# A half tile of w1 shared by pairs of outputs in 64-row tiles, PSUM given out as eight single banks, and norms on two engines

## The chip, the cores and the metric

The kernel runs on one core of a Trainium2 chip. A core has five engines that run their own instruction streams and wait for each other by semaphores: TensorE (PE, matrix products into PSUM), VectorE (DVE), ScalarE (ACT), GpSimd (POOL) and SyncE (SP), which here issues transfers. PSUM, where matrix products end, has eight banks of 128 rows x 512 fp32 values. The metric is the device time of one execution in microseconds; the median of three runs of the kernel before is 190.47 us (190.22 to 190.83).

## What is computed

A block of a transformer over 2048 tokens of width 448, with norms whose scale and shift come from a condition vector. Attention has 16 heads of width 28 and looks at 8 positions, two apart. The MLP has 1792 hidden units. Cut to what matters:

```python
mod = (silu(c) @ w_mod).reshape(1, 6, 1, 448)          # sa, ca, ga, sb, cb, gb
h = layernorm(x) * (1 + ca) + sa
q, k, v = split(h @ wqkv)                               # 16 heads of 28
attn = softmax over idx = pos - 2 * arange(8), masked   # per position
x = x + ga * (attend(attn, v) @ wo)
h = layernorm(x) * (1 + cb) + sb
y = layernorm(h)
x = x + gb * (gelu(y @ w1 + b1) @ w2 + b2)
```

## The kernel before

Tokens are laid out so that even ones come first, then odd ones: the distance of two becomes a distance of one. There are 16 blocks of 128 tokens. The width of 448 makes four k-tiles, the last of them half full: 3 x 128 + 64 rows. The bias b1 stands in row 64 of the last k-tile of `w1_s` (`KA`), against a column of ones in `ybufs`; the rest of that tile is zero.

The whole program is a list of named operations, each with its engine (or a choice of two), a planned duration, what it needs and which buffers it takes. `Plan.order` (L99) walks through them with a planner's clock and always takes the operation that could start first, corrected by priorities (`PRI`, `NUDGE`, `LOOK`). The order of instructions on every engine is what comes out; it is fixed when the program is built. PSUM is three pools with turns in them (`SLOTS`): `lt`, two buffers of two banks, `s`, three of one bank, and `p2`, one bank.

The operations, with their names in the plan and their lines:

- `fst`, `frs`, `z`, `zt`, `h` (`front_end`, L491): statistics of x, 1/sqrt(variance) on GpSimd (L416), the norm (L421, VectorE only), the transposition (L517 on PE for blocks 0 to 7, by a transfer for the rest), scale and shift into `hT` (L526, L529).
- `qk`, `qe` (L539, L386, L384): q and k of two or four blocks, 8 outputs of 4 matmuls, copied out by ScalarE or VectorE.
- `lt`, `ex`, `mk`, `pv`, `ve`, `po`, `rd`, `on`, `pt`, `ot` (`attention`, L598) for each of 17 groups of 121 positions. `lt` is 16 matmuls of 28 rows, placed at row 32*r of the array, into two buffers of two banks; `ex` is two exponentials over 1024 columns each (L624); `mk` masks; `po` multiplies by v; `on` divides.
- `wo`, `x1` (L700, L705): the output product and the addition to x.
- `s2`, `r2`, `z2`, `ml`, `ad`, `s3`, `r3`, `y`, `yt` (`norm_items`, L707): the two norms ahead of the MLP, for pairs of blocks, and a transposing transfer of `ybuf` into `yT` (L739).
- `w1`, `ge` (`mlp_items`, L744), for four chunks of four blocks: 7 steps of two outputs, 4 matmuls of 128 x 512 each (L755), then one gelu over both banks (L762).
- `w2`, `fin`, `out` (L778, L791, L793): the second product, two matmuls a step and block, the additions, and the output transfer.
- `ps_sa`, `ps_ca`, `mod1`, `pb_ga` to `pb_gb` (L453 to L462, L563): the condition's six vectors. Where the last k-tile has 64 rows, matmuls of 64 rows or columns stand between ones of 128.
- `idle` (L325): matmuls on zeros while the first loads are under way.

Of the kernel before, what the change touches and what calls it, by code (L numbers as in the profile page):

```python
# [15 lines left out]
DP = 512  # L16
KT = 4
KA = 64
# [16 lines left out]
SLOTS = {"lt": 2, "s": 3, "p2": 1, "et": 2, "on": 2, "vb": 3, "z2": 2, "yT": 2, "hm": 2}  # L35

LANDS = [("c", 3.0), ("x0", 5.0), ("x2", 5.8), ("wmsa", 6.4), ("wmca", 7.2), ("wk", 8.4), ("wq", 9.4), ("later", 10.0),
         ("wv", 10.4), ("x4", 12.5), ("wmod2", 18.0), ("wo", 19.5), ("b2", 20.5), ("x8", 22.0), ("w1", 28.0),
         ("w2", 33.0)]

NIDLE = [11, 4]
PLANS = None

LOOK = 0.000121

PRI = {"ad": -181.5, "agfst": -82.1, "ags2": -347.3, "ex": -137.9, "ge": -154.4, "h": -94.5, "lt": 209.3,
       "mk": -29.7, "ml": 177.8, "on": -459.2, "po": -127.9, "pv": -157.8, "r2": 73.3, "r3": -46.8, "s2": -114.2,
       "s3": -56.5, "ve": 41.4, "w1": -75.6, "w2": -12.0, "wo": 472.9, "wq": 377.0, "x1": 437.8, "y": -137.1,
       "yt": 24.4, "z": -134.6, "z2": 11.3, "zt": 143.7}

NUDGE = {"ad12": 15.6, "ad2": -30.3, "ad8": 44.8, "agfst12": -48.8, "agfst6": 98.9, "ags2_13": -79.7,
       "ags2_14": 66.3, "ags2_15": -24.2, "ags2_2": 13.3, "ags2_8": 84.1, "ags3_13": 100.2, "ags3_14": -12.2,
       "ex14.1": 144.5, "fin2": 21.9, "ge2.0": -4.6, "ge3.3": -73.9, "h2.2": 280.0, "lt10": 82.1, "lt8": -96.4,
       "mk16": -4.1, "mk3": 236.6, "ml0": 45.3, "ml12": 24.2, "ml6": -123.2, "on16": -89.1, "on4": -65.7,
       "on9": 60.2, "ot11": 20.9, "ot2": 66.5, "ot3": -126.0, "ot4": -23.7, "out1": 36.4, "out14": 29.2,
       "out15": -322.5, "out2": 24.7, "out9": -87.4, "po16": 38.4, "po9": 49.4, "pt16": 16.3, "pt2": 36.7,
       "pt3": -118.5, "pv13": -326.1, "pv16": 12.1, "qe0.0": 77.8, "qe0.6": -60.5, "qe12.5": 124.2,
       "qe2.5": 111.3, "qe8.0": 142.3, "qe8.3": 117.4, "qk2.5": 255.7, "qk8.0": 142.4, "qk8.1": 138.6,
       "r2_10": 7.9, "r2_12": 207.3, "r2_14": 18.8, "r2_14a": 2.8, "r2_4a": 155.1, "r2_8": -68.9, "r2_8a": 87.6,
       "r3_0a": -13.7, "r3_10a": -65.1, "r3_12": -63.0, "r3_12a": 43.9, "r3_14": 28.5, "r3_14a": -10.2,  # L60
       "r3_8": -10.6, "rd15": 41.6, "rd16": -89.1, "s2_1": 61.5, "s2_12": -57.7, "s2_13": -42.9, "s2_15": -4.9,
       "s2_3": 68.8, "s2_9": -35.4, "s3_12": 65.1, "s3_14": 46.0, "w1_0.6": 31.3, "w1_1.5": 58.9,
       "w1_3.3": -59.1, "w2_0.6": 121.6, "w2_1.4": 61.0, "w2_11.0": 60.4, "w2_11.3": -105.2, "w2_11.4": -4.4,
       "w2_11.5": 45.1, "w2_11.6": 30.7, "w2_12.5": -140.6, "w2_13.2": -158.9, "w2_14.1": -6.6, "w2_14.3": -1.2,
       "w2_14.4": 47.8, "w2_14.5": 147.1, "w2_2.5": 20.1, "w2_4.2": -47.2, "w2_5.2": -7.0, "w2_5.3": -24.7,
       "w2_5.5": 19.2, "w2_5.6": -17.6, "w2_6.1": 3.9, "w2_6.2": 12.3, "w2_6.6": 5.9, "w2_8.0": -68.8,
       "w2_8.3": -69.5, "w2_8.5": 91.6, "w2_9.3": 69.1, "wo1": 88.2, "wo12": -28.3, "wo2": 44.1, "x1_1": 34.4,
       "x1_13": -39.6, "x1_3": -114.7, "y1": 51.8, "y10": 10.9, "y12": 102.0, "y13": -21.9, "y14": 13.4,
       "y3": 128.0, "yt12": -52.1, "yt13": 30.6, "yt14": 12.1, "yt9": 260.3, "z2_1": 79.9, "z2_12": 15.9,
       "z2_13": 66.8, "z2_14": 106.9, "z2_15": 45.5, "z2_4": 123.4, "z2_6": -29.2}  # L70
# [9 lines left out]
class Plan:  # L80
# [8 lines left out]
    def add(self, name, eng, needs=(), after=(), uses=(), allocs=(), lag=0.09, tab=None, at=0.0, fn=None, pri=0.0):  # L89

        i = len(self.ops)
        self.index[name] = i
        self.ops.append(dict(name=name, eng=eng, needs=list(needs), after=list(after), allocs=list(allocs), lag=lag,
                             tab=tab, at=at, fn=fn, pri=pri + PRI.get(re.match(r"[a-z]+([0-9](?=_))?", name)[0], 0.0) +
                             NUDGE.get(name, 0.0)))
        for b in list(uses) + list(allocs):
            self.bufs[b][1].append(i)

    def order(self, hop=0.07, table=1.3, win=3.413):  # L99
# [27 lines left out]
        tab = None  # L127
# [6 lines left out]

        def slot_time(t, extra=0):
            k = len(turn[t]) + extra - self.slots[t]
            if k < 0:
                return 0.0
            b = turn[t][k] if k < len(turn[t]) else None
            if b is None or any(end[u] is None for u in users[b]):  # L140
                return None
            return max(end[u] for u in users[b]) + hop

        while ready:
            best = None
            for i in ready:
# [7 lines left out]
                ok, cntt = True, {}  # L154
                for b in o["allocs"]:
                    tg = tag_of[b]
                    st = slot_time(tg, cntt.get(tg, 0))
                    cntt[tg] = cntt.get(tg, 0) + 1
                    if st is None:
                        ok = False  # L160
                        break
                    t = max(t, st)
# [4 lines left out]
                s = max(t, free[e])  # L167
# [3 lines left out]
                if best is None or key < best[0]:  # L171
                    best = (key, i, e, s)
            assert best is not None, [ops[i]["name"] for i in ready]
            _, i, e, s = best
            o = ops[i]
            d = o["eng"][e]
            if e == "PE":
                w = int(s / win)
# [11 lines left out]
            for b in o["allocs"]:  # L190
                turn[tag_of[b]].append(b)
# [14 lines left out]
def kernel(  # L206
# [39 lines left out]

    cst = ctx.enter_context(tc.tile_pool(name="cst", bufs=1))
    ps_lt = ctx.enter_context(tc.tile_pool(name="ps_lt", bufs=2, space=bass.MemoryType.PSUM))
    ps_s = ctx.enter_context(tc.tile_pool(name="ps_s", bufs=SLOTS["s"], space=bass.MemoryType.PSUM))
    ps_p2 = ctx.enter_context(tc.tile_pool(name="ps_p2", bufs=SLOTS["p2"], space=bass.MemoryType.PSUM))  # L250

    def ps_att(shape, dtype, name):
        return ps_s.tile(shape, dtype, name=name, tag="s")

    ps_small = ps_att
# [35 lines left out]
    b2_bc = cst.tile([128, D], BF16, name="b2_bc")  # L291
    silu_bf = cst.tile([128, KT], BF16, name="silu_bf")
# [9 lines left out]
    wmod = stp.tile([128, KT, 2, D], BF16, name="wmod")  # L302
    wqk_st = stp.tile([128, KT, 2 * D], BF16, name="wqk_st")
    nc.scalar.dma_start(out=x_all[:, 0:2, :], in_=xv[:, 0, 0:2, :])
    load_ktiles(nc.sync, wmod[:, :, 0, :], w_mod[:, 0:D], 0)
    load_ktiles(nc.scalar, wmod[:, :, 1, :], w_mod[:, D:2 * D], 0)
# [7 lines left out]
    nc.sync.dma_start(out=b2_bc[:], in_=B_b2.partition_broadcast(128))  # L314
    nc.sync.dma_start(out=x_all[:, 8:NBLK, :], in_=xv[:, 1, :, :])
# [6 lines left out]
    def idle(n):  # L322
        for i in range(n):
            idle_ps = ps_att([128, 512], FP32, "idle_ps")
            nc.tensor.matmul(idle_ps[:], lhsT=idle_in[:, 0:128], rhs=idle_in[:], start=True, stop=True)  # L325

    idle(4)
# [5 lines left out]
    nc.vector.memset(w1_s[64:128, KT - 1, :], 0.0)  # L333
# [26 lines left out]
    c_col = stp.tile([128, KT], FP32, name="c_col")  # L360
# [3 lines left out]
    nc.vector.memset(c_col[:], 0.0)  # L364
    nc.gpsimd.memset(share[:], 1.0 / 64)
    nc.vector.memset(ca1_col[64:128, KT - 1:KT], 0.0)
    nc.vector.memset(sa_col[64:128, KT - 1:KT], 0.0)
    for vb in vbufs:
        nc.gpsimd.memset(vb[:, :, DH:DH + 1], 1.0)
    for yb in ybufs:  # L370
        nc.gpsimd.memset(yb[:, D:DP], 0.0)
        nc.gpsimd.memset(yb[:, D:D + 1], 1.0)
    load_ktiles(nc.sync, w1_s, B_w1, 0)
    nc.sync.dma_start(out=w1_s[KA:KA + 1, KT - 1, :], in_=B_b1.rearrange("(o n) -> o n", o=1))
# [35 lines left out]
    def rstd(nm, tile_key, n, **kw):  # L410
        def a_fn(e):
            tv = T["tv", tile_key] = sm.tile([128, n], FP32, name="tv", tag=f"tv{n}")
            nc.vector.tensor_scalar_add(out=tv[:], in0=T["mv", tile_key][:, :, 1], scalar1=EPS)  # L413
        def fn(e):
            rs = T["rs", tile_key] = sm.tile([128, n], FP32, name="rs", tag=f"rs{n}")
            nc.gpsimd.tensor_tensor(out=rs[:], in0=T["tv", tile_key][:], in1=neg_half[:, 0:n], op=ALU.pow)  # L416
        P.add(nm + "a", {"DVE": 0.08}, fn=a_fn, **kw)
        P.add(nm, {"POOL": 0.75}, lag=0.02, needs=[nm + "a"], fn=fn)

    def normalize(dst, src, tile_key, i):  # L420
# [10 lines left out]
    def c_fn(e):  # L431
        T["ps_c"] = ps_s.tile([128, KT], FP32, name="ps_c", tag="s")
# [14 lines left out]
    def col_fn(v):  # L447
        if v == 0:
            T["ps_col"] = ps_s.tile([128, 2 * KT], FP32, name="ps_col", tag="s")
        for j in range(KT):  # L450
            nj = kr_of(j)
            for kt in range(KT):
                nc.tensor.matmul(T["ps_col"][0:nj, v * KT + j:v * KT + j + 1],  # L453
                                 lhsT=wmod[0:kr_of(kt), kt, v, j * 128:j * 128 + nj],
                                 rhs=silu_bf[0:kr_of(kt), kt:kt + 1], start=(kt == 0), stop=(kt == KT - 1))

    def mod1_fn(e):
        ps_col = T["ps_col"]
        nc.vector.tensor_scalar_add(out=ca1_col[:, 0:KT - 1], in0=ps_col[:, KT:2 * KT - 1], scalar1=1.0)
# [400 lines left out]
```

## Time and profile before

| | |
|---|---|
| median of the runs | 190.47 us (190.22 to 190.83) |
| the profiled execution, its own time | 190.52 us |
| its span, first to last instruction | 188.8 us |
| first qk matmul | 13.28 us |
| matmuls of w1 (L755) | 224, two outputs a step |
| matmuls of w2 (L778) | 224 |
| exponentials (L624) | 34 of 1024 columns, 1029 ns |
| gelus (L762) | 28 of 1024 columns, 1024 ns |
| powers on GpSimd (L416) | 21, mean 954 ns |

PE is TensorE's matmuls and PEld its weight loads; DVE, ACT, POOL and SP are VectorE, ScalarE, GpSimd and SyncE. A matmul's mean duration holds its way through the pipeline, so the time that one takes in a stream is read from the chain or from busy time divided by the count. The page also cuts the span into 40 slices and gives the busy share of each in tenths:

```profile
PE   7989899899999898999999999999999999999993
DVE  5688799996998999967989998399999602202451
ACT  3048687587777866558744575868364444251100
PEclk9969999999999999999999999999999999999999
```

### The profile page before, as it was taken

The numbers are of one execution on the slowest core, as the hardware profiler recorded it, in microseconds if no ns is written. First come the engines' busy times: TensorE is split into PE (matmuls) and PEld (weight loads), VectorE is DVE, ScalarE is ACT, GpSimd is POOL, SyncE is SP. The second block draws the span as 40 slices with busy tenths as digits, with TensorE's granted clock in tenths as the row PEclk, the third lists the DMA queues.
The fourth block names the chain that finished last, engine by engine and source line by source line (L and its number), as shares of the span: only waits on it lengthen the run. The fifth ranks groups of instructions, "written<-read, shape, count | busy, mean of one in ns | idle before, by whom it ended". The sixth has DMA issues, their size and how long they took to land.

```text
span 188.8 us, 3664 instructions
## 1 busy us (share of the span) xinstructions
PE 179.8 (95%) x1446; PEld 94.5 (50%) x1460; DVE 140.3 (74%) x344; ACT 105.4 (56%) x149; POOL 23.7 (13%) x53
## 2 busy tenths in 40 slices
PE   7989899899999898999999999999999999999993
PEld 2658644445544444445556544456554444444551
DVE  5688799996998999967989998399999602202451
ACT  3048687587777866558744575868364444251100
POOL 7132002200104100311030103100103100000000
PEclk9969999999999999999999999999999999999999
DMA  5999992541001150004013002120000220000021
GB/s 178 302 375 295 406 309 89 111 83 33 0 3 28 28 61 0 0 0 59 24 43 65 0 28 53 32 50 3 26 30 28 54 56 24 3 24 0 28 70 49
DMA packets 23285, 14.40 MB, mean 76 GB/s; under 512 B 13666, under 2 KB 22371, under 8 KB 23268
## 3 DMA queue, kind: packets, MB, share of 16 engines
q1 hardware_dynamic: 22244, 13.31, 26.6%
q10 hardware_dynamic: 1024, 0.86, 1.4%
q8 instruction: 11, 0.18, 0.4%
q14 instruction: 6, 0.05, 0.1%
HBM read 9.18 MB, written 1.84 MB: 58 GB/s over the span
## 4 chain that ended last, share of the span: by engine, by line
PE 72%; DVE 15%; DMA 5%; POOL 2%; issue 2%; ACT 1%; ACTq 1%; DVEq 0%
PE p L755 25%; PE p L778 23%; PE pw L700 6%; DVE st L396 5%; PE pv L648 4%; PE pq L539 4%; DMA x_all<-in_A_x_dram 3%; PE lt L613 2%; PE pt L679 2%; POOL rs L416 2%; PE po L658 2%; DMA yT<-ybuf 2%; PE ptr L517 1%; DVE hT L529 1%; DVE zbuf L421 1%
## 5 line engine op out<-in xcount | busy, mean ns | idle before, releaser
L755 PE MATMUL p<-yT,w_s 128*128 128x512 bf16 x216 | 50.5, 379 | 1.1 <-DMA yT<-ybuf 0.7
L778 PE MATMUL p<-w_s,hm 128*128 128x448 bf16 x224 | 48.3, 352 | 0.1
L762 ACT ACTIVATE hm<-p 128x1024 bf16<-128x1024 f32 x28 | 28.6, 1024 | 31.6 <-PE p L755 29.5
L624 ACT ACTIVATE et<-lt 128x1024 bf16<-128x1024 f32 x34 | 33.9, 1029 | 9.1 <-PE lt L613 9.1
L416 POOL TENSOR_TENSOR rs<-tv,neg_half 128x2 f32<-128x2 f32 (+1 forms) x21 | 20.0, 954 | 125.1 <-DVE tv L413 102.5
L755 PEld LDWEIGHTS <-w_s 128*128 128x128 bf16 x224 | 21.6, 98 | 25.9 <-issue 1.1
L778 PEld LDWEIGHTS <-hm 128*128 128x128 bf16 x224 | 21.1, 98 | 19.0
L539 PE MATMUL pq<-hT,Wqk 128*128 128x512 bf16 (+1 forms) x155 | 29.2, 335 | 0.8 <-DVE qT L384 0.6
L791 DVE TENSOR_TENSOR xt<-p,gbb_bc 128x448 f32<-128x448 f32 x11 | 6.8, 622 | 27.0 <-PE p L778 26.9
L539 PEld LDWEIGHTS <-Wqk 128*128 128x128 bf16 x160 | 15.3, 98 | 12.0 <-issue 1.1
L633 DVE TENSOR_TENSOR et<-et,mask_rest 128x2048 bf16<-128x2048 bf16 x17 | 20.6, 1209 | 0.2 <-ACT et L624 0.2
L396 DVE BATCH_NORM_STATS2 st<-x_all 128x6 f32<-128x448 bf16 x30 | 17.8, 615 | 1.6 <-DMA x_all<-in_A_x_dram 1.4
L700 PE MATMUL pw<-wo_s,oT 128*128 128x448 bf16 x64 | 14.8, 353 | 0.5 <-ACT oT L386 0.3
L648 PE MATMUL pv<-Wv,hT 128*128 128x448 bf16 x68 | 15.0, 353 | 0.0
L386 ACT CAST kT<-pq 128x512 bf16<-128x512 f32 (+1 forms) x19 | 9.6, 508 | 4.6 <-PE pq L539 4.1
L705 DVE TENSOR_TENSOR x_all<-pw,x_all 128x448 bf16<-128x448 f32 x16 | 9.8, 615 | 2.5 <-PE pw L700 2.3
L669 DVE TENSOR_TENSOR on<-po,rden 128x448 bf16<-128x448 f32 x17 | 10.5, 619 | 0.1
L386 ACT CAST vbuf<-pv 128x448 bf16<-128x448 f32 x15 | 7.8, 538 | 4.7 <-PE pv L648 4.7
L658 PEld LDWEIGHTS <-et 128*128 128x128 bf16 x272 | 9.0, 96 | 2.6 <-DVE x_all L705 0.2
L386 ACT CAST qT<-pq 128x512 bf16<-128x512 f32 (+1 forms) x18 | 9.1, 526 | 1.7 <-PE pq L539 1.2
L658 PE MATMUL po<-vbuf,et 128*128 128x29 bf16 x272 | 9.3, 176 | 0.0
L396 DVE BATCH_NORM_STATS2 st<-z 128x6 f32<-128x448 bf16 x16 | 9.2, 615 | 0.1
(101 smaller groups left out, 165.5 us busy)
## 6 DMA issues: line engine op xcount, KB each, us to landing
out_dram<-x_all SPq DMA_DIRECT2D x16, 112.0 KB, 1.7
w_s<-in_B_w_dram SPq DMA_DIRECT2D x1, 1568.0 KB, 13.4
wmod<-in_w_mod_dram SPq DMA_DIRECT2D x1, 1344.0 KB
w_s<-in_B_w_dram SPq DMA_DIRECT2D x1, 1344.0 KB, 14.4
x_all<-in_A_x_dram SPq DMA_DIRECT2D x1, 896.0 KB, 10.8
wqk_st<-in_A_wqkv_dram SPq DMA_DIRECT2D x2, 336.0 KB
x_all<-in_A_x_dram ACTq DMA_DIRECT2D x2, 224.0 KB, 4.3
x_all<-in_A_x_dram SPq DMA_DIRECT2D x1, 448.0 KB, 5.2
```

The costliest lines, as they stand in the source:

```text
L386: nc.scalar.copy(out=out, in_=in_)
L396: nc.vector.bn_stats(out=st[:], in_=src())
L416: nc.gpsimd.tensor_tensor(out=rs[:], in0=T["tv", tile_key][:], in1=neg_half[:, 0:n], op=ALU.pow)
L539: nc.tensor.matmul(pq[:, 0:w], lhsT=Wqk[:, kt, m, :], rhs=hT[:, kt, c0:c0 + w], start=(kt == 0), stop=(kt == KT - 1))
L624: nc.scalar.activation(out=et_v[:, 2 * half:2 * half + 2], in_=T["lt", g][half][:].rearrange("p r (ft c) -> p r ft c", ft=4), func=ACT.Exp ...
L633: nc.vector.tensor_tensor(out=et[:], in0=et[:], in1=mask_rest[:], op=ALU.mult)
L648: nc.tensor.matmul(pv[:], lhsT=hT[:, kt, k0:k0 + BK], rhs=Wv[:, kt, :], start=(kt == 0), stop=(kt == KT - 1))
L658: nc.tensor.matmul(po[:, h, :], lhsT=T["et", g][:, h, :], rhs=vbufs[g % NVB][:, h, :], start=True, stop=True)
L700: nc.tensor.matmul(pw[:], lhsT=oT[:, kt, jb * 128:(jb + 1) * 128], rhs=wo_s[:, kt, :], start=(kt == 0), stop=(kt == KT - 1))
L755: nc.tensor.matmul(p1[:, f, 0:w], lhsT=w1_s[:, kt, ft * 128:(ft + 1) * 128], rhs=T["yT", c][:, kt, 0:w], start=(kt == 0), stop=(kt == KT - 1))
L762: nc.scalar.activation(out=T["hm", c][:, 2 * q:2 * q + 2, 0:w], in_=T["p1", c, q][:, :, 0:w], func=ACT.Gelu_apprx_tanh)
L778: nc.tensor.matmul(T["p2", b][:], lhsT=T["hm", c][:, ft, bi * 128:(bi + 1) * 128], rhs=w2_s[:, ft, :], start=(ft == 0 and b not in XPE), s ...
```

## The change

**w1.** The width of 448 is now read as 128 + 128 + 128 + 64 in a way that two outputs can share: k-tiles 0 to 3 hold rows 0-127, 128-255, 192-319 and 320-447. `load_twice` loads w1 so, and `twice` makes the norm write y so (512 columns, 64 of them twice). The first output of a pair takes tiles 0, 3, 1 whole and the rows 256-319, which are the upper half of tile 2; the second takes 0, 3, 2 whole and the rows 128-191, which are the lower half of tile 1. Each output has three full matmuls (`mains`) and one of 64 rows (`ends`), at array rows 64-127 and 0-63. `ends` of two pairs go together (operation `wt`). b1 moves from the row of w1 to a column that gelu adds; a transposition of 14 rows makes it (`b1_fn`).

```diff
+    def mains(outs, lhs, rhs):
+        for w, o in enumerate(outs):
+            for i, kt in enumerate((0, 3, 1 + w)):
+                nc.tensor.matmul(o, lhsT=lhs(w, slice(0, 128), kt), rhs=rhs(slice(0, 128), kt), start=(i == 0),
+                                 stop=False)
+    def ends(outs, lhs, rhs):
+        for w, (o, r, kt) in enumerate(zip(outs, (slice(64, 128), slice(0, 64)), (2, 1))):
+            nc.tensor.matmul(o, lhsT=lhs(w, r, kt), rhs=rhs(r, kt), start=False, stop=True)
...
-                p1 = T["p1", c, q] = ps_lt.tile([128, 2, 512], FP32, name="p1", tag="lt")
-                for f in range(2):
-                    ft = 2 * q + f
-                    for kt in range(KT):
-                        nc.tensor.matmul(p1[:, f, 0:w], lhsT=w1_s[:, kt, ft * 128:(ft + 1) * 128],
-                                         rhs=T["yT", c][:, kt, 0:w], start=(kt == 0), stop=(kt == KT - 1))
+                mains([ps_of(nm, w) for nm in p1s], lhs_of(q), rhs)
...
+            if q % 2 or q == FT // 2 - 1:
+                qs = [q - 1, q] if q % 2 else [q]
+                def t_fn(e, qs=qs):
+                    for q in qs:
+                        ends([ps_of(f"p1_{c}.{ft}", w) for ft in (2 * q, 2 * q + 1)], lhs_of(q), rhs)
```

**PSUM.** The three pools become eight tiles of one bank. The planner chooses a bank for each buffer (`choose`: the one that comes free first), knows a cost for changing the number of rows (`turn_over`), and lets at most two `p2` be open. An exponential now reads one bank, 512 columns, four to a group; a gelu one output, with b1 as its bias.

```diff
-SLOTS = {"lt": 2, "s": 3, "p2": 1, "et": 2, "on": 2, "vb": 3, "z2": 2, "yT": 2, "hm": 2}
+SLOTS = {"p2": 2, "et": 2, "on": 2, "vb": 3, "z2": 2, "yT": 2, "hm": 2}
...
+    psum = [pool.tile([128, 512], FP32, name=f"ps{i}") for i in range(8)]
+    def ps_of(nm, n=512):
+        return psum[P.bank[nm]][:, 0:n]
...
-        for half in range(2):
-            def x_fn(e, half=half):
+        for r in range(4):
+            def x_fn(e, r=r):
...
+            nc.scalar.activation(out=T["hm", c][:, ft, 0:w], in_=ps_of(f"p1_{c}.{ft}", w),
+                                 func=ACT.Gelu_apprx_tanh, bias=b1_col[:, ft:ft + 1])
```

**Norms.** `z`, `z2` and `y` may run on ScalarE as well, as scale and bias; for that VectorE negates the mean and GpSimd multiplies it by the inverse deviation, for every norm.

```diff
+            nc.vector.tensor_scalar_mul(out=ng[:], in0=T["mv", tile_key][:, :, 0], scalar1=-1.0)
...
+            nc.gpsimd.tensor_tensor(out=nb[:], in0=T["nm", tile_key][:], in1=rs[:], op=ALU.mult)
...
+        if e == "ACT":
+            nc.scalar.activation(out=dst, in_=src, func=ACT.Identity, bias=T["nb", tile_key][:, i:i + 1],
+                                 scale=T["rs", tile_key][:, i:i + 1])
+            return
```

**The condition.** `wmod` and `wmod2` are filled up with zeros to 128 rows (and `wmod` to 512 columns), so that the matmuls of L453 and L563 all have 128 rows; `mod1` and the product of `wo_s` with ga take fewer instructions. The zero matmuls of the start are split differently:

```diff
-NIDLE = [11, 4]
+NIDLE = [8, 3, 3, 4]
```

**The order.** The landing times that the planner is told (`LANDS`), `LOOK`, `PRI` and `NUDGE` are new, so operations come in another order on every engine. Seen in the order of instructions: on PE the first eight qk matmuls stand ahead of the second pair's transpositions, and the number of outputs and groups is the same. Up to the first gelu ScalarE has 36 exponentials (of 512 columns) instead of 18 (of 1024), 8 norms, and 6 of the 8 copies into `Wqk`, which VectorE had. The two statistics that ScalarE did (L399 to L402) go to VectorE.

## The prediction

> **What bounds the kernel now.** I read the page's first part, then the busy time in two stretches, then the chain of waits, then the groups by shape.
>
> ```profile
> PE 179.8 (95%) x1446; PEld 94.5 (50%) x1460; DVE 140.3 (74%) x344; ACT 105.4 (56%) x149; POOL 23.7 (13%) x53
> ...
> 8.00:72.00 64.00, 59.96 (x595) 34.02 (x601) 58.22 (x154) 46.23 (x76) 8.88 (x8) 0.97 0.51 141
> ...
> 71.40:185.70 114.30, 113.81 (x825) 58.01 (x833) 77.34 (x169) 58.20 (x71) 10.40 (x12) 1.00 0.13 30
> 185.70:188.80 3.10, 0.00 (x0) 0.00 (x0) 0.59 (x1) 0.00 (x0) 0.00 (x0) 1.00 0.11 37
> ```
>
> The columns of the stretches are length, then busy time of PE, PEld, DVE, ACT and POOL, then the granted clock. From 71.4 us, where the first w1 matmul stands, to 185.7 us PE is idle for only 0.5 us of 114.3 at full clock: there every microsecond taken out of PE's stream comes off the end. From 8 to 72 us three engines share the load (PE 60, DVE 58, ACT 46 of 64), so PE's sum is not the limit there. The last 3.1 us are one VectorE addition and the output transfer.
>
> ```profile
> 37.37 0.86 PE pb_sb L563 x4
> 38.22 0.86 PE pv L648 x4
> 39.09 0.34 PE lt L613 x16
> 39.42 0.86 PE pw L700 x4
> ...
> 67.97 3.29 DMA yT<-ybuf
> 71.39 0.38 PE p L755
> ...
> 84.27 0.76 PE pw L700 x4
> ...
> 158.27 0.38 PE p L778 x2
> 158.65 1.73 PE p L755 x8
> ```
>
> This is the chain that ended last: start, length, what. Eight w1 matmuls take 1.73 us, 0.216 each; four of 448 columns take 0.76 (0.189 each), but 0.86 behind an lt group. An lt group is 16 matmuls of 28 rows in four row tiles; it takes 0.34, and one after the other they would take 16 x 0.055 = 0.88 (pt's four 128-column ones take 0.22). So row tiles do run side by side: four waves are 0.22 us, and 0.12 is left for entering the mode, 0.10 for leaving it (0.86 - 0.76). The pb_sb line shows the same for 64 rows: its last matmul has 64, and it and the pv behind it each take 0.86 where 0.76 is due. A change of row mode costs 0.10 us.
>
> **PE's stream, part by part.** Old w1: 28 pairs of outputs in four chunks, 8 matmuls each, 224 x 0.216 = 48.4 us. New: 6 full matmuls a pair (168 x 0.216 = 36.3) and two 64-row ones on different row tiles. Side by side a pair of those takes 0.216, so 28 x 0.216 = 6.05; one after the other 12.1. No row shows 64-row pairs; the nearest, lt's four tiles, ran side by side, so I take 6.05: 6.05 us removed. The upper bound is nothing removed.
>
> The 64-row matmuls come in 4 x 4 = 16 groups. In the instruction order of the two kernels I counted the changes between 128, 64 and 32 rows from the first qk on: 34 round lt before, 64 after (two groups stand directly beside an lt), so 30 x 0.10 = 3.0 us added. The four pb groups lose their 64-row matmul: 4 x 0.20 = 0.8 less. The one bias transpose of 14 rows replaces the bias row; I give it 0.05, with pt's 0.055 beside it. Sum over PE: -6.05 + 3.0 - 0.8 + 0.05 = -3.8 us.
>
> The page TensorEngine Tiling (Array Packing) of the Trainium skill, section Key Properties, says that changing the tiling mode, not just the tile, drains the engine, which speaks against 30 more changes. The drain is in the 0.10 us measured above. With the constant of about 166 ns that TensorE: Matmul & The Clock Gate gives under Single matmul latency as an estimate for each change, the 3.0 would be 5.0 and the whole forecast 2.0 us later.
>
> What counts is how this splits at the first w1. Priced with the rows above, PE's work from the first qk (13.28 us) to the first w1 is 53.5 us before and 54.2 after: pb gives back 0.8, and about 1.0 us of po, wo and pt groups and 8 ptr transposes (0.46) stand ahead of w1 that stood elsewhere. PE has 58.1 us for its 53.5 there, so this is covered; if the cover goes, 0.7 us is the price. Behind the first w1 it is 113.8 us before (114.3 measured) and 109.8 after: -4.0 us (-6.05 + 3.0 - 1.0 moved ahead). This goes to the end whole.
>
> **When the first w1 starts.** It waits for yT, that for the last y of its four blocks, and that stands in VectorE's stream, which is the chain for most of 22 to 35 and 46 to 66 us. I counted VectorE's instructions up to that y in both orders. Gone: 6 of 8 Wqk copies (0.22 each, 1.3 us), 4 z and 2 y to ScalarE (6 x 0.36 = 2.1), an hT and a qT piece (0.4 each), half of the small ca and sa operations (0.3), the second wo_s piece (0.1): 4.6. Added: 9 negations of the mean (0.165 each, 1.5), one vbuf copy (0.6), one 512-wide hT (0.5), one more mask product that now stands ahead (1.2), the bias column (0.15): 4.0. Net -0.6 us.
>
> ```profile
> L624 ACT ACTIVATE et<-lt 128x1024 bf16<-128x1024 f32 x34 | 33.9, 1029 | 9.1 <-PE lt L613 9.1
> L386 ACT CAST kT<-pq 128x512 bf16<-128x512 f32 x12 | 7.0, 586 | 3.6 <-PE pq L539 3.4
> L421 DVE TENSOR_SCALAR z<-x_all,mv,rs 128x448 bf16<-128x448 bf16 x16 | 5.6, 392 | 0.8 <-POOL rs L416 0.6
> L526 ACT ACTIVATE hT<-ptr,sa_col,ca_col 128x512 bf16<-128x512 bf16 x2 | 1.6, 778 | 1.6 <-DVE hT L529 1.1 <-PE ptr L517 0.5
> ```
>
> These are groups by shape: busy time, mean of one, idle time ahead and its releaser. ScalarE pays for all this. An exp or gelu over one bank isn't in the trace; the nearest 512-wide read of PSUM takes 0.58 busy, half of 1029 would be 0.51, and the two-operand form 0.78. I take 0.58. Up to the first gelu: 36 exps instead of 18 (20.9 - 18.0 = 2.9), 8 norms at 0.70 (between the 0.538 of a 448-wide copy and 0.78) 5.6, 6 Wqk copies at 0.54 3.2, the small exchanges about nothing. That is +11.7 on 46.2 of 64 us, 91% busy. At 72% VectorE waited for ScalarE 1.1 us (hT) and 0.2 (et) in this stage; I add half as much again, +0.6, against VectorE's -0.6. So the start stays at 71.4. Low bound: the first z no longer stands behind the second pair's statistics, which wait for x2 until 8.3 us; rs was there by 7.65 and z came at 9.46, so -1.8 more, -2.4 in all. High bound: ScalarE ends the stage, below.
>
> ScalarE: Activation LUTs of the skill, section What ACT_TABLE_LOAD costs, has an ACTIVATE with a pointer bias at about 280 ns + 0.833 a column. By that estimate a 512-wide gelu takes 0.71, and 56 of them 7 us more ScalarE time than mine; the trace's 1024-wide row, 1.024 us, lies below that page's 1.13.
>
> After 71.4 us ScalarE has 58.2 of 114.3 us to do; gelu adds 56 x 0.58 - 28.6 = 3.9, exp 2.6, the four later norms 2.8, and the two statistics that leave it take off 4.1. It stays near 63 of 110, hidden by PE. Two gelus take 1.16 us while PE spends 1.6 on a pair (12 x 0.216 + 0.43 + 0.20 for two pairs). GpSimd's second product per norm (21 more at its 0.7 to 1.1 us) follows the power on a queue 13% busy, and only ScalarE's norms wait for it: nothing, if ScalarE's norms have room, else 0.9 us a norm in the opening. The w1 load has 64 rows more; the loads of w1 and w2 were issued from 11.7 to 17.6 us, landed some 14 us later and are used from 71 on, so 35 us of slack hide it. On SP one small bias load (0.4 to 0.6 us of issue, as its neighbours) stands ahead of x8's, whose statistics are first read at 26.5 us behind 2 us of wo_s work; without that cover it costs 0.6. The memsets change places: w1's (0.8 us on VectorE) for two of wmod (0.48 for the like of 64x512, and a narrow one), ybuf's eight on GpSimd for one of wmod2, all ahead of the first statistics or on an idle queue: nothing.
>
> **Sum.** Start of w1 0, stream behind it -4.0, bubbles (0.5) and the tail (3.1) as before: the span goes from 188.8 to 184.8. The profiled execution took 190.52 with 1.7 us round its span, and the median is 190.47, so the two need no correction: 190.5 - 4.0 = 186.5 us. Its own range is 184.1 (w1 2.4 earlier) to 188.5 (w1 two later).
>
> **Rivals.** (1) ScalarE becomes the bound of the opening. For it: 91% busy by the sum, in-order, with four exps ahead of each mask product. Against it: it still has 6 us free. If it ends the stage, w1 starts some 3 us late (half of the 6 us free, and 0.07 more on each of 36 exps would do it): 189.5. (2) The 64-row pairs do not run side by side, because the second's weights come after the first has streamed: nothing removed, 30 changes paid, 186.5 + 6.05 = 192.5, slower than before. It decides from a lag of 0.14 us between the two starts (4.0 / 28). Against it: lt's 16 matmuls in 0.34. (3) Banks: pairs stay open across two groups and hold four of eight banks until gelu has read them, in an order fixed beforehand. Now w1 waits for no reader in the trace (0.1 us idle ahead of L778, 1.1 of L755, of it 0.7 yT). If each of the 28 pairs waits 0.14 us for a bank, the gain is gone: 190.5.
>
> **How the numbers follow.** Forecast 0.62, rival 1 0.16, rival 2 0.08, rival 3 0.14. A measurement tells 0.3% apart, so below 189.9 is faster and above 191.0 slower. Faster: 0.62, 0.12 of rival 1, 0.04 of rival 3, 0.78. The same: 0.02 and 0.05, 0.07. Slower: 0.02, rival 2's 0.08, 0.05, 0.15. The range goes to 183.6 below, where the early w1 meets half of the bubbles, and to 190.2 above, past rival 1 and short of rival 2.
>
> **What would show it.** The pairs: two 64-row w1 matmuls starting within 0.05 us, four of them with the changes at 0.63 us. The changes: 0.10 on the group behind each. The opening: first w1 between 69 and 73.4 us, ScalarE about 58 us busy from 8 to 72. Behind it: about 110 us of PE with under 1 us idle. I am wrong if w1's start moves by more than 2.4 us, if an exp of one bank takes over 0.65, or if PE waits for bank readers behind 72 us.

## The result, and the profile after

The changed kernel takes 182.24 us (median of four runs, 181.71 to 182.44); the kernel before, run beside it, 190.65 us (190.22 to 191.73). The ratio is 0.955 (0.950 to 0.959). The profiled span went from 188.8 to 180.5 us, 8.3 us less, where 4.0 were forecast: the sign is right and half of the gain was not foreseen.

The first part of the page of the changed kernel, and its slices:

```profile
PE 174.4 (97%) x1464; PEld 88.4 (49%) x1464; DVE 138.4 (77%) x348; ACT 118.6 (66%) x217; POOL 32.7 (18%) x67
...
PE   6989999999999999999999999999999999999992
...
DVE  5789899799998999997989988688879865020251
ACT  2298996999898946999578475995835810077400
...
PEclk9999999999999999999999999999999999999999
```

PE is at 90% or more from the fourth slice to the last but one; before, it dropped to 8 in five slices of the first twenty. The stretches of the changed kernel (length, then busy time of PE, PEld, DVE, ACT and POOL, the granted clock, DMA):

```profile
8.00:72.00 64.00, 62.90 (x628) 35.01 (x625) 59.94 (x158) 54.43 (x109) 12.81 (x19) 1.00 0.49 144
...
11.76:66.44 54.68, 54.52 (x571) 31.30 (x571) 51.62 (x135) 48.07 (x99) 9.97 (x14) 1.00 0.50 145
...
66.44:177.30 110.86, 110.40 (x826) 52.93 (x825) 78.31 (x178) 65.37 (x109) 16.34 (x24) 1.00 0.13 31
...
177.30:180.50 3.20, 0.00 (x0) 0.00 (x0) 0.62 (x1) 0.00 (x0) 0.00 (x0) 1.00 0.10 36
```

The same view of the kernel before, from its first qk to its first w1:

```profile
13.28:71.39 58.11, 54.68 (x554) 30.43 (x557) 52.74 (x130) 44.14 (x73) 7.18 (x7) 1.00 0.46 123
```

The first w1 came at 66.44 us instead of 71.39 (4.95 earlier; the forecast had 0), and from there to the last w2 it takes 110.86 us instead of 114.3 (3.45 less; the forecast had 4.0). In the opening PE has about the same work, but it was idle for 3.43 of 58.11 us before and is idle for 0.16 of 54.68 now; and its stream of qk starts 1.5 us earlier. Those two make up the 4.95.

Part of the earlier start may be the clock of PE and not the order. In the profiled execution of the kernel before, PE was granted 0.50 of its clock from 10 to 13 us (0.97 from 8 to 72 us); in that of the changed kernel it was granted 1.00 there. Over the executions of the kernel before that ran beside the experiments, 12 with a mean granted clock of 1.00 have a median of 190.2 us, 30 with 0.99 one of 190.6, and five with 0.98 one of 192.2. The changed kernel's four executions had 1.00 (one 0.999). By the first two medians the clock is worth about 0.4 of the 8.4 us; why it falls in some executions isn't shown here.

What PE waited for in that stretch (line waited for, total, times, longest), in the kernel before:

```profile
PE pt L679 <- DVE on L669: 1.2, 2, 0.9
PE pq L539 <- DVE qT L384: 0.6, 1, 0.6
PE pw L700 <- ACT oT L386: 0.3, 1, 0.3
PE pw L700 <- ACT vbuf L386: 0.2, 1, 0.2
```

These are 2.3 of the 3.43 us; another 1.1 stand ahead of the first w1 itself, 0.7 of them for yT. In the changed kernel one wait is left, ahead of the stream at 11.76 us:

```profile
PE ps L599 <- ACT Wqk L436: 0.9, 1, 0.9
```

The chain of the changed kernel (start, length, what):

```profile
10.79 0.46 ACT hT L586
11.26 0.46 ACT Wqk L436
...
11.76 0.81 PE ps L599 x6
12.57 0.57 PE ps L577 x8
...
65.72 0.76 PE ps L623 x4
66.48 2.72 PE ps L295 x12
69.19 0.76 PE ps L763 x4
69.95 0.54 PE ps L300 x4
70.49 2.70 PE ps L295 x12
...
124.17 2.59 PE ps L295 x12
```

Where the chain before w1 was VectorE's norm and the transposing transfer, it now runs through PE itself: the last of the condition's products ends, and w1 begins. L300 is the four 64-row matmuls of two pairs: 0.54 us, with the entry into their mode. Twelve full ones (L295) behind them take 2.70 where 12 x 0.216 = 2.59 are due, which is what the twelve at 124.17 behind full ones take: 0.11 for leaving it. (The very first twelve, at 66.48, take 2.72 with no change of mode just ahead; why isn't shown.)

Groups by shape (busy time, mean of one, idle time ahead) of what moved to ScalarE and GpSimd:

```profile
L689 ACT ACTIVATE et<-ps 128x512 bf16<-128x512 f32 x68 | 36.1, 613 | 3.3 <-PE ps L678 3.0 <-ACT ybuf L477 0.2
L812 ACT ACTIVATE hm<-ps,b_col 128x512 bf16<-128x512 f32 x56 | 34.1, 692 | 23.2 <-PE ps L300 23.1
...
L477 ACT ACTIVATE ybuf<-z,nb,rs 128x512 bf16<-128x512 bf16 x5 | 3.9, 807 | 3.1 <-POOL nb L471 3.1
...
L477 ACT ACTIVATE zbuf<-x_all,nb,rs 128x448 bf16<-128x448 bf16 x4 | 3.0, 761 | 3.5 <-POOL nb L471 3.4
...
L471 POOL TENSOR_TENSOR nb<-ng,rs 128x2 f32<-128x2 f32 x18 | 7.1, 394 | 1.4
```

ScalarE waits for PE ahead of the gelus (23.1 us): it is not what ends anything behind the first w1.

### The profile page after: what moved, and what is told of

It reads as the page before. It is cut to its first block, busy times and chain, and to the rows that moved or that the text cites. A ratio compares the mean times of both kernels' runs of the same rounds, so it can differ in the third digit from the quotient of the medians.

```text
span 180.5 us, 3837 instructions
## 1 busy us (share of the span) xinstructions
PE 174.4 (97%) x1464; PEld 88.4 (49%) x1464; DVE 138.4 (77%) x348; ACT 118.6 (66%) x217; POOL 32.7 (18%) x67
## 3 DMA queue, kind: packets, MB, share of 16 engines
q10 hardware_dynamic: 1024, 0.86, 1.5%
## 4 chain that ended last, share of the span: by engine, by line
PE 72%; DVE 12%; DMA 4%; ACT 4%; SPq 2%; issue 2%; ACTq 1%; POOL 1%; DVEq 0%
PE ps L295 21%; PE ps L853 20%; PE ps L599 8%; PE ps L763 6%; PE ps L711 5%; PE ps L300 4%; DVE st L446 4%; DMA hT<-zbuf 3%; PE ps L721 3%; PE ps L678 2%; DVE et L696 2%; PE ps L742 2%; SPq L803 2%; DVE hT L589 2%; DMA yT<-ybuf 1%
## 5 line engine op out<-in xcount | busy, mean ns | idle before, releaser
L812 ACT ACTIVATE hm<-ps,b_col 128x512 bf16<-128x512 f32 x56 | 34.1, 692 | 23.2 <-PE ps L300 23.1
L853 PE MATMUL ps<-w_s,hm 128*128 128x448 bf16 x224 | 47.2, 353 | 0.0
L295 PE MATMUL ps<-yT,w_s 128*128 128x512 bf16 x168 | 39.5, 380 | 0.5 <-DMA yT<-ybuf 0.5
L689 ACT ACTIVATE et<-ps 128x512 bf16<-128x512 f32 x68 | 36.1, 613 | 3.3 <-PE ps L678 3.0
L599 PE MATMUL ps<-hT,Wqk 128*128 128x512 bf16 (+1 forms) x160 | 31.3, 337 | 0.9 <-ACT Wqk L436 0.9
L295 PEld LDWEIGHTS <-w_s 128*128 128x128 bf16 x168 | 15.5, 98 | 21.9 <-issue 5.3
L711 PE MATMUL ps<-Wv,hT 128*128 128x448 bf16 x68 | 15.7, 353 | 0.0
L763 PE MATMUL ps<-wo_s,oT 128*128 128x448 bf16 x64 | 14.1, 352 | 0.0
L768 DVE TENSOR_TENSOR x_all<-ps,x_all 128x448 bf16<-128x448 f32 x16 | 9.7, 619 | 3.1 <-PE ps L763 3.0
L436 ACT CAST qT<-ps 128x512 bf16<-128x512 f32 (+1 forms) x19 | 9.6, 518 | 2.0 <-PE ps L599 1.5
L732 DVE TENSOR_TENSOR on<-ps,rden 128x448 bf16<-128x448 f32 x17 | 10.5, 616 | 0.2
```

The source lines that it names most:

```text
L295: nc.tensor.matmul(o, lhsT=lhs(w, slice(0, 128), kt), rhs=rhs(slice(0, 128), kt), start=(i == 0), stop=False)
L436: nc.scalar.copy(out=out, in_=in_)
L599: nc.tensor.matmul(pq, lhsT=Wqk[:, kt, m, :], rhs=hT[:, kt, c0:c0 + w], start=(kt == 0), stop=(kt == KT - 1))
L689: nc.scalar.activation(out=et_v[:, r], in_=T["lt", g][r].rearrange("p (ft c) -> p ft c", ft=4), func=ACT.Exp, scale=float(DH) ** -0.5)
L711: nc.tensor.matmul(pv, lhsT=hT[:, kt, k0:k0 + BK], rhs=Wv[:, kt, :], start=(kt == 0), stop=(kt == KT - 1))
L763: nc.tensor.matmul(pw, lhsT=oT[:, kt, jb * 128:(jb + 1) * 128], rhs=wo_s[:, kt, :], start=(kt == 0), stop=(kt == KT - 1))
```

## The experiments

The question after the result: the stream behind w1 fell nearly as priced, so what took PE's waits out of the opening? Theory A: the norms on ScalarE and the Wqk copies relieve VectorE, whose results PE waited for. Theory B: the eight single banks let PE run ahead of the readers. Theory C: the new landing times and the new order alone. Beside these, the two prices of the pairs were measured by themselves. In kernels marked "planned anew", the planner's priorities were looked for again for that structure, with the planner's own clock as the judge; the others keep the order of the kernel that they come from.

**The pairs, alone.** Both 64-row matmuls of a pair made full, so that there is no change of mode; 64 rows of w1 enter each output twice:

```diff
-        for w, (o, r, kt) in enumerate(zip(outs, (slice(64, 128), slice(0, 64)), (2, 1))):
+        for w, (o, r, kt) in enumerate(zip(outs, (slice(0, 128), slice(0, 128)), (2, 1))):
```

> The 56 closing matmuls of w1 take all 128 rows, so each adds 64 rows of w1 a second time; order, banks and everything else as after. If the 64-row pairs ran side by side and a change of row mode costs 0.10 us: PE gets 28 x 0.216 = 6.05 us more and 30 changes fewer (3.0), so 182.2 + 3.0 = 185.3 us, first w1 unmoved at 66.5. If the pairs had run one after the other: 182.2 - 3.0 = 179.2.

Measured: 185.87 us (184.79 to 186.67), ratio 0.976 (0.971 to 0.980), 3.6 us above the changed kernel. Its chain:

```profile
70.37 0.76 PE ps L763 x4
71.13 0.86 PE ps L300 x4
71.99 2.59 PE ps L295 x12
```

Four full matmuls take 0.86 and the ones behind them 0.216 each. Against 0.54 + 0.11 that is 0.21 for a group of two pairs, 12 x 0.21 = 2.5 us; the four groups of one pair hardly differ (0.43 against 0.32 + 0.11). The other microsecond is the opening: in this execution the first w1 came at 67.6 instead of 66.4 with the same order, so the start moves by about 1 us between executions, and differences in it of that size mean little.

Both on the same row tile, so that the modes change but nothing runs side by side; the rows of the second are the wrong half of w1:

```diff
-        for w, (o, r, kt) in enumerate(zip(outs, (slice(64, 128), slice(0, 64)), (2, 1))):
+        for w, (o, r, kt) in enumerate(zip(outs, (slice(64, 128), slice(64, 128)), (2, 1))):
```

> Both closing matmuls of a pair use rows 64 to 127 (the second takes the other half of its k-tile, so 64 rows of w1 are other ones than they should be); the number of mode changes stays. Side by side before: now one after the other, 28 x 0.216 = +6.05, 188.3 us, and a group of four takes about 0.97 instead of 0.54. One after the other before already: no change, 182.2.

Measured: 188.26 us (188.25 to 188.55), ratio 0.989 (0.986 to 0.992), 6.0 above the changed kernel. Its chain:

```profile
69.27 0.76 PE ps L763 x4
70.03 0.97 PE ps L300 x4
71.00 2.70 PE ps L295 x12
```

0.97 instead of 0.54, and the same 0.11 behind (a single pair takes 0.54 instead of 0.32): on one tile the four run one after the other, on two tiles two at a time. The first w1 stands at 66.5. What the pairs save by lying side by side is 12 x 0.43 + 4 x 0.22 = 6.0 us.

**The norms, order kept.** The norms and the Wqk copies that ScalarE had are issued by VectorE at their places in the order:

```diff
     todo = P.order()
+    for o in P.ops:
+        if re.fullmatch(r"(z|z2_|y)[0-9]+|w[qk][01]", o["name"]):
+            o["ran"] = "DVE"
```

> The norms (z, z2, y) and the Wqk copies that the plan gave to ScalarE are issued on VectorE at their planned place; the order of all else and the banks stay. Theory A, the opening was shortened because ScalarE took work off VectorE: first w1 goes from 66.5 back to 69.5 or later, time 185 or more. Theory B, it was the eight free banks, or C, the order: first w1 moves by under 1 us, time under 183.5.

Measured: 184.1 us (183.89 to 185.57), ratio 0.968 (0.964 to 0.973): 1.9 above the changed kernel. The order was made for norms on ScalarE, so part of that can be the order's. The first w1 stands at 67.8, between what theories A and B had led to expect, and its chain is VectorE's again:

```profile
62.27 1.13 DVE et L696
63.40 0.65 DVE ybuf L480 x2
64.05 0.30 DVE kT L434
...
65.04 2.63 DMA yT<-ybuf
67.67 0.14 issue
67.81 0.81 PE ps L295 x3
```

**The norms, planned anew.** The same structure as the changed kernel, with no choice of engine for the norms:

```diff
-... {"DVE": 0.32, "ACT": 0.65} ...
+... {"DVE": 0.32} ...
-... {"DVE": 0.35, "ACT": 0.7} ...
+... {"DVE": 0.35} ...
```

> After, but z, z2 and y run on VectorE only, planned and searched anew (the Wqk copies may still go to ScalarE). Theory A, norms on ScalarE shortened the opening: first w1 later than 68.5, time 184.5 or more. If a plan made for it can do without: first w1 by 67.7, time within 1.2 us of 182.2.

Measured: 184.2 us (183.68 to 184.57), ratio 0.966 (0.963 to 0.969), first w1 at 68.4. The new order doesn't get the 2.0 us back. But a search of this kind also came out 1.4 us above the changed kernel with the norms on both engines ("measured durations", below), so only about 0.6 of the 2.0 is clear of the search.

**The banks.** First all buffers were held to pools like the old ones, with the changed kernel's priorities:

```diff
-            return min(((max(t, bt[k]), k) for k in range(8) if bt[k] is not None and k not in taken), default=None)
+            own = range(7) if nm.startswith("p1") else range(4) if nm.startswith(("lt", "ptr")) else \
+                (7,) if nm.startswith("p2") else range(4, 7)
+            return min(((max(t, bt[k]), k) for k in own if bt[k] is not None and k not in taken), default=None)
```

> The planner may choose banks only as the old pools had them: lt and ptr among four, p2 one, all other buffers of the opening among three (w1 any of the seven); the plan is made anew with the same priorities. Theory B, banks: first w1 comes 3 us or more later than 66.5, time 185 or more. Theory A: first w1 within 1 us, time within 1.5 us of 182.2. A plan made anew also shifts the order, so up to 1 us says nothing.

Measured: 217.11 us, ratio 1.140. The last qk moved to 86.8 us, behind the first w1 at 72.4: the priorities belong to a structure and give a bad order with another. That says nothing about banks. So w1 was let into every bank, w2's buffer into four, and the kernel planned anew:

```diff
+            own = range(8) if nm.startswith("p1") else range(4) if nm.startswith(("lt", "ptr")) else \
+                range(4, 8) if nm.startswith("p2") else range(4, 7)
```

> After, but up to the first w1 the banks are given out only as the old pools had them (lt and ptr four, all else three; w1 may take any, p2 one of four), priorities searched anew. Theory B, the eight free banks shortened the opening: first w1 at 68.5 us or later, time 184.5 or more. If not: first w1 within 1.2 us of 66.5 (which is how far it moved between executions so far); the time may then still be a little over 182.2, since p2 has fewer banks too.

Measured: 187.91 us (186.86 to 189.64), ratio 0.987 (0.980 to 0.994). The first w1 stands at 68.1, and between the first qk and it PE waits for readers of banks (line waited for, total, times, longest):

```profile
PE ps L683 <- DVE kT L406: 1.6, 1, 1.6
PE ps L571 <- ACT qT L408: 1.0, 1, 1.0
PE ps L683 <- ACT qT L408: 0.6, 1, 0.6
```

Behind w1 it is longer too, 114.0 instead of 110.9 us, but mostly because more of PE's work stands there: 113.1 us busy instead of 110.4, and 0.9 idle instead of 0.5. The median hides two groups: the two executions at a granted clock of 1.00 took 186.9 and 187.0 us, the two at 0.99 188.8 and 189.6. Against the first two the limit costs 4.7 us.

**Both taken back.** The two edits before this together, planned anew:

> After with both parts of the opening taken back: z, z2 and y on VectorE only, and banks up to the first w1 only as the old pools gave them; priorities searched anew. If the norms (1.9 us of first w1 so far) and the banks (1.7) are two causes that add: first w1 at 70 us or later, PE idle between first qk and first w1 4 us or more, 187.9 + 2 = 189.9 us. If they are one cause seen twice: first w1 at 68.5, time 188.

Measured: 186.62 us (186.49 to 187.21), ratio 0.980 (0.976 to 0.983), 4.4 above the changed kernel and less than either theory had led to expect. The first w1 stands at 69.4: 3.0 later than in the changed kernel, less than 2.0 and 1.7 together. In this execution PE waits 1.6 us for the transfer of yT ahead of the first w1, and at most 0.8 for readers of banks. The two don't add: with the banks limited, taking the norms' second engine back costs nothing more (186.6 against 186.9 and 187.0 at the same clock).

**The order.** Four operations moved in the kernel before, so that the first z doesn't wait behind the second pair's statistics:

```diff
     todo = P.order()
+    ahead(["frs0", "z0", "z1"], "fst2")
+    ahead(["mod1"], "wk0")
```

> The kernel before, its order kept but for VectorE's start: the first two norms stand ahead of the second pair's statistics (which wait for x2) and the condition's columns ahead of the Wqk copies. Theory C, the opening was short of truth in the planned order: first hT about 1.0 us earlier than 11.30, first qk and with them part of the first w1 (71.4) too, time 189.5 or less. Rival: another wait takes its place before the first w1, which stays within 0.3 us of 71.4, time 190.5.

Measured: 190.38 us, ratio 0.999 (0.997 to 1.001); first qk at 13.4. The first norm came 1.8 us earlier (7.70 instead of 9.46) and the first hT 1.0 (10.32 instead of 11.30), but not the first qk: on PE the second pair's transpositions stand ahead of it, and they wait for that pair's norm, which waits until 12.2 us for GpSimd's power (2.2 us from 9.96). In the changed kernel eight qk matmuls stand ahead of these transpositions.

The kernel before with the changed kernel's landing times (`LANDS`, x of the second pair at 8.3 instead of 5.8 among them), planned anew:

> The kernel before (three PSUM pools, two-bank exponentials, norms on VectorE, eight w1 matmuls a pair) planned anew with the landing times of after (x2 at 8.3 instead of 5.8 us), its priorities searched anew for the planner's clock. Theory C, the opening was long because the order was planned for loads that land otherwise: first w1 near 68 us or earlier and time 187.5 or less. Rival A or B, the norms or the banks are needed: first w1 stays at 70.5 or later, time 189.5 or more.

Measured: 190.74 us (190.05 to 192.27, ten runs), ratio 1.002 (0.999 to 1.006). The first qk came at 11.7 and the first w1 at 70.7, but the time stayed: landing times and an order found for them gain nothing in the old structure, so theory C alone isn't the answer.

The kernel before with those landing times and the norms' second engine, planned anew:

```diff
+            nc.vector.tensor_scalar_mul(out=ng[:], in0=T["mv", tile_key][:, :, 0], scalar1=-1.0)
...
+            nc.gpsimd.tensor_tensor(out=nb[:], in0=T["nm", tile_key][:], in1=rs[:], op=ALU.mult)
...
-            P.add(f"z{b}", {"DVE": 0.32}, ...
+            P.add(f"z{b}", {"DVE": 0.32, "ACT": 0.65}, ...
```

> The kernel before with the norms' choice of ScalarE alone added (with the negated mean and the second GpSimd product), the landing times of after, priorities searched anew; three PSUM pools and 224 full w1 matmuls as before. If ScalarE's norms shorten the opening by themselves: first w1 about 2 us ahead of the 70.7 that the same kernel had with norms on VectorE only, time about 188.7. If they do so only together with the eight banks: first w1 at 70 or later, time 190 or more.

Measured: 190.04 us (189.49 to 191.03, ten runs), ratio 0.998 (0.995 to 1.001). In the old pools the norms' second engine is worth about half a microsecond (0.7 against the kernel just above; the interval reaches from nothing to 1.0).

**Towards a better one.** The changed kernel with the measured durations told to the planner (norms 0.76 and 0.81 on ScalarE, gelu 0.61), planned anew:

```diff
-... {"DVE": 0.32, "ACT": 0.65} ...
+... {"DVE": 0.36, "ACT": 0.76} ...
-... {"ACT": 0.58} ...
+... {"ACT": 0.61} ...
```

> After, with the planner told the durations that ScalarE and VectorE had in its profile (norm 0.76 and 0.36, y 0.81 and 0.40, gelu 0.61) and priorities searched anew. If the true durations make a better order: under 181.5. If the order of after is as good as such a search gets, or its finer steps matter more: 182 or more.

Measured: 183.6 us (183.15 to 183.85), ratio 0.963 (0.959 to 0.966), 1.4 above. Its first w1 is the earliest of all, 65.6, but from there to the last w2 it takes 113.3 us: work left out ahead of w1 comes behind it. Nothing was taken back here, so the 1.4 us are what this search gives away against the order of the changed kernel.

The last three pairs of a chunk closed in one group of six, 12 groups instead of 16, planned anew:

```diff
-            if q % 2 or q == FT // 2 - 1:
-                qs = [q - 1, q] if q % 2 else [q]
+            if q in (1, 3, 6):
+                qs = [4, 5, 6] if q == 6 else [q - 1, q]
```

> After, but the last three pairs of a chunk are closed in one group of six 64-row matmuls instead of four and two: 12 groups instead of 16, planned and searched anew. By the price of a change (0.21 us a group in and out) PE gets 4 x 0.21 = 0.84 us less: 181.4 us, with a group of six at about 0.75. If six open banks make w1 or others wait for banks, or the order found is no better: 182.2 or more, with more PE idle behind the first w1 than after's 0.5.

Measured: 184.03 us (183.68 to 184.45), ratio 0.965 (0.962 to 0.969), 1.8 above. The group of six takes 0.76 us, so the four groups saved are saved, but the first w1 came at 67.4 and the stretch behind it took 111.4: the order that was found lost more than that. No version ran faster than the changed kernel.

**The runs side by side.** The span is the start of qk's stream, PE's work from there, PE's idle time from there, and the tail. In us, from the profiled executions in which PE's records are complete (the kernel before lacks 14 of 1,460 matmuls; the one with four operations moved has the same structure and all of them):

| kernel | qk from | PE work | PE idle | tail | span |
|---|---|---|---|---|---|
| before, four operations moved | 13.4 | 169.2 | 3.4 | 3.2 | 189.2 |
| before, new landing times | 11.7 | 170.3 | 3.7 | 3.2 | 188.9 |
| before, those and norms on two engines | 11.0 | 170.4 | 3.4 | 3.2 | 188.0 |
| after, norms and banks taken back | 12.1 | 165.8 | 3.8 | 3.2 | 184.9 |
| after, banks taken back | 10.5 | 166.4 | 5.2 | 3.2 | 185.3 |
| after, norms taken back | 11.2 | 165.5 | 2.8 | 3.2 | 182.7 |
| after, measured durations | 11.3 | 165.5 | 2.1 | 3.2 | 182.1 |
| after | 11.8 | 164.9 | 0.6 | 3.2 | 180.5 |

The lines with the old pools have 3.4 to 5.2 us of idle PE, whatever the order and the norms. Free banks with the norms on VectorE leave 2.8; both together leave 2.1 in one order and 0.6 in that of the changed kernel. An earlier qk alone buys nothing: where it came 1.7 earlier in the old structure, PE's work from there grew by 1.1 and its idle time by 0.3. By the forecast's price of eight transpositions, 0.46 of the 1.1 is the second pair's, which then stand behind the first qk. In the first two rows PE was granted 0.50 of its clock for some of the time from 10 to 13 us, in the others 1.00.

## Why the prediction was half right

**The pairs and the changes of mode: right.** Side by side they take 0.54 for four with the entry and 0.11 behind, 0.65 against the 0.63 forecast; the 6.05 us were 6.0 when the pairs were put on one tile. The lt groups of 28 rows were a good guide to 64 rows. The constant of 166 ns from TensorE: Matmul & The Clock Gate (Single matmul latency) would, as an estimate for each change, have made a group some 0.13 us dearer; the runs keep the 0.10 of the rows. That a change of mode costs at all, as TensorEngine Tiling (Array Packing) has it under Key Properties, they confirm.

**PE's work: right to 0.6 us.** From the first qk on it fell from 169.2 to 164.9 us, or 165.3 with two qk matmuls that stand alone at 10.3 us: 3.9 less. The forecast's two parts from there make 3.3 (its 3.8 leaves out eight transpositions, 0.46, that now stand behind the first qk). The work ahead of w1 was to grow by 0.7 and stayed the same (54.9 us by the complete records, 54.5 + 0.4 after). Behind w1 the work was to fall by 4.0 and fell by 3.8 (114.2 to 110.4 by the complete records); the stretch itself fell by 3.45, since PE waits 0.5 us for yT there.

**"So the start stays at 71.4": wrong, and the step that failed.** In the sum this is "Start of w1 0"; it measured -4.95 us. The first w1 came at 66.44, below the low bound of 69.0 as well. The step took VectorE's stream as the limit of the opening, found its sum only 0.6 us shorter, set 0.6 of waits for ScalarE against it, and stopped. Two things were wrong in it. VectorE's busy time indeed hardly fell (52.74 to 51.62 us), but PE had 58.1 us for its work, and the difference was read only as cover that could hide 0.7 us of more work. It was idle time in the middle of the chain, made of waits in turns between PE, VectorE and ScalarE, and it could go too: some 3 us of it did. And the norms and the free banks were priced by engine sums, at nothing together. Taken back together, in an order searched anew, they cost 4.4 us, of which such a search can account for about 1.4; what is left without them is 186.6 us, where the forecast said 186.5. Some of that agreement is chance, since qk starts 1.2 us earlier there and PE's work is 0.9 longer than in the changed kernel.

**The low bound: wrong for a like reason.** It gave 1.8 us to an earlier first z. Moving that z in the kernel before brought the 1.8 at z and nothing at the first qk, which stood behind the second pair's transpositions. qk's earlier start comes with the order, in which it no longer does: with the norms and the copies put back on VectorE at the same places it still came at 11.3, and at 10.5 to 12.1 in what was planned anew.

**The rivals.** ScalarE as the bound (1) didn't come: 54.4 us busy from 8 to 72, where 58 were forecast. Its exps took 0.53 (36.1 / 68) instead of 0.58, 1.8 us less on 36 of them; norms of 0.76 to 0.81 instead of 0.70 took back 0.7; the rest isn't split. Pairs in series (2) is what the kernel with one tile shows, 188.3 us, and it isn't what happens. Bank waits behind w1 (3) didn't come: PE is idle for 0.46 of 110.86 us there, all of it at yT. The banks mattered in the other direction and in the other stage, the opening, where the forecast had no line for them.

**Open.** Between the old structure with new landing times (first w1 at 70.7) and the new one with norms and banks taken back (69.4) lie the single-bank exps, the zero-filled condition weights and the copies on ScalarE; they weren't separated. Nor is the share of norms, banks and order known well, since an order planned anew with nothing taken back came out 1.4 us slower than the changed kernel's. The norms are worth between about 0.6 (2.0 less 1.4) and 1.9 us, the latter in an order that was made for ScalarE's norms. The banks stand better: 4.7 us at full clock, some 3 with the search taken off. That the order of the changed kernel itself is a third cause is likely by these numbers, but no run tested it by itself.

## What to carry to other kernels

Where several engines share a stage, ask not which sum falls, but how long the most loaded engine is idle there and how late it starts: of the 3.4 us of idle time here the change took out 3.3, and it started the stream 1.5 earlier. Try a buffer limit and a second engine for the same chain together: either alone left 2.8 to 5.2 us of idle PE, both left 0.6 in one order and 2.1 in another, so the order has to be found with them. Prices from neighbouring rows (a change of mode, side-by-side tiles) held to a few hundredths; the priorities of a tuned order don't hold for another structure.

## What was new of the hardware

- An exponential over one bank of 512 columns costs 0.53 us in its stream (36.1 / 68), against 1.0 for two banks (33.9 / 34): halving 34 of them added 2.2 us in all.
- A gelu over 512 columns with a pointer as bias costs 0.61 (34.1 / 56). By the estimate from ScalarE: Activation LUTs (What ACT_TABLE_LOAD costs) one would take 0.71, and the mean of one, 692 ns, is close to that; the 93 ns by which the same section has back-to-back ones overlap lead to the 0.61.
- GpSimd's product of two columns takes 0.39 us (x18), far below the power ahead of it (0.95).
- Four 64-row matmuls over 512 columns take 0.54 us on two row tiles and 0.97 on one, four of 128 rows 0.86, each as the chain shows them behind full ones.
